# Gate logits as four more columns of A's key projection, read out by GpSimd and spread through DRAM

## The chip, the core and the metric

The kernel runs on one core of a Trainium2 chip. The metric is the device time of one execution in microseconds (us). The kernel is written in Bass with the Tile framework: the program names tiles and engines, the framework adds the semaphore waits that its view of the tiles' reads and writes asks for.

Engines, as the profile names them: PE (TensorE matmuls; PEld its weight loads), DVE (VectorE), ACT (ScalarE), POOL (GpSimd), SP (SyncE, which here only issues transfers). Each executes its instructions in program order. Sums of matmuls land in PSUM, everything else is kept in SBUF.

## What is computed

Two linear-attention blocks, A and B, on the same `x` (2048 rows, 640 columns, 32 heads of 20), mixed by a gate per row:

```
phi(t) = where(t > 0, t + 1, exp(t)) + 1e-6
q, k, v = split(x @ wqkv)               # per block, 32 heads
kv  = phi(k)^T v ;  z = sum over rows of phi(k)
o   = phi(q) kv / (phi(q) z + 1e-6)
block = o @ wo
g   = sigmoid(sum(x * gate_w))          # one logit per row
out = g * A + (1 - g) * B
```

All inputs and the output are bf16.

## The kernel before

The kernel never forms v. It takes G = x^T phi(k) (640x640), then kv = wv^T G per head, multiplies by wo to a 640x640 matrix M per block, and the output is phi(q) M for both blocks, with phi(q) already scaled by the gate and by the reciprocal of the denominator. Rows are taken in 16 chunks of 128 (`ST`), columns in 5 tiles of 128 (`DT`, index c).

The gate comes in through `ge`: geA = 1 + exp(-logit) and geB = 1 + exp(logit). The denominator of block b is multiplied by ge[b] before its reciprocal (L492), which makes the scale of phi(q) equal to g/den for A and (1-g)/den for B. `gate_pass` (L176) makes `ge`: for each half of the rows 20 small matmuls with the gate vector copied to 32 weight columns (`gwr`), in four column groups of PE, so that each group of 32 partitions holds the logits of 256 rows, 32 times over; then two exponentials on ACT and two additions on DVE. That is the layout in which `rec_pass` has the denominators.

Order of work for block A, on the parts that matter here:

- Loads. x's first 512 rows come as four chunks (`load_x`, from SP and ACT), wkA as c = 0, 1, 2 and 3 to 4 together (`load_wk`), then wqA, then the other rows of x by transposing DMAs on SP.
- `k_first` (L222), its order written out by hand: PE transposes the first two x chunks, DVE copies them to xT, PE does k's matmuls of these two chunks for c = 0 and 1, transposes the third chunk, does c = 2 and the third chunk's c = 0 to 2, transposes the fourth, and finishes. `k_mm` does one matmul of 320 columns: a chunk of k has two halves (`hf`), each in a PSUM bank of its own.
- `phi` (L194) takes k or q out of PSUM: ACT writes exp into the tile `e` (three buffers), DVE does min and add on it in place (L200), then add and max with the PSUM source into `pk` or `pqT` (L204). In a "lifted" unit ACT also writes t + 1 into the destination (L199), and DVE's last step reads that instead of PSUM (L202).
- The other k chunks and the q units (`q_unit`, 10 matmuls of 512 columns) alternate; the last part, under a manual schedule, is k chunks 14 and 15, `gwr` widened by DVE between them (L702), then five q units (`q_pass`), of which the last four are lifted, with sums of pk by DVE between (`k_sum`).
- `g_pass` (L278): 32 matmuls of the last c of G. After 12 of them come `z_rows` (z from the sums of pk, 16 matmuls named zA at L388, and DVE's `zr` at L396), `x_sum(1)` (DVE, L502) and `gate_pass` (matmuls named lg); after 14 more `z_pass` (5 matmuls, then DVE's `zsel` at L407). `rec_pass` then makes the denominators (denA) with `zsel` as weights. After it come the rest of G (`g_strassen`) and block B's k, q and G, which go the same way; `ge` is made once and used by both.

PSUM has four slots (`ps`), each of two banks. Without a number, `ps` takes the next slot of a round-robin (`turn`); `g_pass`, `z_rows`, `gate_pass`, `rec_pass` and `g_strassen` name slots 1, 0, 2, 2 and 0/1. Late in the kernel `D3` receives differences of phi(q), from the middle of block B's k stage on (`p_diff`).

SP's queue holds, in order: x, wk and wq loads, 15 transposing loads, the gate vector (640 elements, one to a partition and column), x again in row order, wvA, woA, wkB (waits until A's k is done), wqB (waits until A's q is done), and later transfers.

## Time and profile before

| what | value |
|---|---|
| runs shown | 189.83 us median of 3 (189.77 to 190.37) |
| profiled execution | span 188.1 us, first to last instruction, 3574 instructions; no time of its own is listed beside the span |
| median of the runs less that span | 1.7 us |
| PE / DVE / ACT / POOL busy | 182.7 / 150.3 / 75.0 / 2.8 us |
| granted PE clock over the span | 1.000 |
| matmuls lg (gate logits) | 40, on the chain for 1.09 us from 52.06 us |
| gate exponentials (ACT), additions (DVE) | 2 of 0.60 us, 2 of 0.42 us |

The page of a profile gives the busy time of each engine in the whole span, the span in 40 slices, the chain of work that ended last (followed back from the last instruction to what released each step), the costliest groups of instructions, and the transfers with their time from issue to landing. The trace behind it can be asked for a timeline of a stretch, for the groups by shape, and for who waited for whom. In a timeline a line is: start, length (us), engine, line of the kernel, operation, output<-inputs, shape, count, and in brackets the idle time before it with what ended it. Matmuls overlap, so the pace of a row of them is read from the length of the row by its count and not from the duration of one.

### The profile page before, as it was taken

Reading aid. Unit: us, or ns where it says so; the run is one execution under the profiler, and the core shown is the slowest. Engines: PE = TensorE matmul, PEld = TensorE weight load, DVE = VectorE, ACT = ScalarE, POOL = GpSimd, SP = SyncE. Lnnn points to the kernel's source line nnn. Section 1 sums busy time; section 2 is a strip of 40 time slices with the busy share of each in tenths; the row PEclk is TensorE's granted clock in tenths of the full one; section 3 lists DMA queues with packets and bytes.
Section 4 is the critical chain, followed back from the end, with each engine's and each line's share of the span. In section 5 each row is a group of like instructions: output and inputs, shape, how many; then the busy total and the mean of one; then the engine's idle time right before and its main releaser. Section 6 shows DMA issues by size and latency. Waiting matters only on the chain.

```text
span 188.1 us, 3574 instructions
## 1 busy us (share of the span) xinstructions
PE 182.7 (97%) x1460; PEld 123.5 (66%) x1465; DVE 150.3 (80%) x244; ACT 75.0 (40%) x106; POOL 2.8 (2%) x17
## 2 busy tenths in 40 slices
PE   8899999999999999999999999999999999999992
PEld 3566657755577677877765555576778776777772
DVE  1378968899998999799889997739699989787553
ACT  2055446457942501367674577422401611111110
POOL 6000000000000000000000000000000000000000
PEclk9999999999999999999999999999999999999999
DMA  5975447992140000011115000000543003211222
GB/s 184 320 124 94 105 84 250 360 249 87 16 164 0 3 0 0 3 33 33 54 44 189 2 0 0 3 0 0 178 112 62 3 3 112 97 70 56 87 71 71
DMA packets 19802, 15.63 MB, mean 83 GB/s; under 512 B 9546, under 2 KB 19658, under 8 KB 19786
## 3 DMA queue, kind: packets, MB, share of 16 engines
q1 hardware_dynamic: 18922, 14.59, 29.0%
q10 hardware_dynamic: 864, 0.82, 1.3%
q8 instruction: 11, 0.18, 0.4%
q14 instruction: 5, 0.04, 0.1%
HBM read 10.00 MB, written 3.44 MB: 71 GB/s over the span
## 4 chain that ended last, share of the span: by engine, by line
PE 93%; DMA 3%; DVE 1%; ACTq 0%; issue 0%; ACT 0%; DVEq 0%
PE gs L325 16%; PE kB L207 12%; PE qB L256 11%; PE kA L207 11%; PE qA L256 7%; PE ox L563 6%; PE oy L563 5%; PE oz L563 5%; PE qA L267 5%; DMA xn<-in_A_x_dram 3%; PE ow L563 3%; PE gB L298 2%; PE gA L298 2%; DVE osb L568 1%; PE mA L456 1%; PE mid L417 1%
## 5 line engine op out<-in xcount | busy, mean ns | idle before, releaser
L207 PEld LDWEIGHTS <-xT 128*128 128x128 bf16 x320 | 31.0, 98 | 12.4 <-DVE xT L192 0.5
L200 DVE TENSOR_SCALAR e<-e 128x640 bf16<-128x640 bf16 (+1 forms) x52 | 18.7, 360 | 6.3 <-ACT e L197 5.7
L207 PE MATMUL kB<-wkB,xT 128*128 128x320 bf16 x160 | 23.0, 299 | 0.0
L207 PE MATMUL kA<-wkA,xT 128*128 128x320 bf16 x160 | 22.6, 299 | 0.1
L256 PE MATMUL qB<-xT,wqB 128*128 128x512 bf16 x98 | 21.7, 379 | 0.1
L197 ACT ACTIVATE e<-kB 128x640 bf16<-128x640 f32 x16 | 11.3, 704 | 18.8 <-PE kB L207 17.5
L256 PEld LDWEIGHTS <-wqB 128*128 128x128 bf16 x100 | 11.7, 117 | 9.8 <-issue 0.2
L197 ACT ACTIVATE e<-kA 128x640 bf16<-128x640 f32 x16 | 11.0, 704 | 13.3 <-PE kA L207 13.3
L204 DVE SCALAR_TENSOR_TENSOR pk<-kA,e 128x640 bf16<-128x640 f32 x16 | 13.2, 825 | 1.7
L204 DVE SCALAR_TENSOR_TENSOR pk<-kB,e 128x640 bf16<-128x640 f32 x16 | 13.2, 825 | 1.7
L197 ACT ACTIVATE e<-qA 128x1024 bf16<-128x1024 f32 x10 | 10.2, 1023 | 9.3 <-PE qA L267 3.7
L197 ACT ACTIVATE e<-qB 128x1024 bf16<-128x1024 f32 x10 | 10.2, 1023 | 8.7 <-PE qB L256 8.4
L256 PE MATMUL qA<-xT,wqA 128*128 128x512 bf16 x59 | 13.2, 379 | 0.1
L607 ACT COPY u<-ox 128x320 f32<-128x320 f32 x8 | 3.4, 425 | 21.9 <-PE ox L563 21.9
L325 PEld LDWEIGHTS <-S 128*128 128x128 bf16 x96 | 9.4, 98 | 3.6
L325 PEld LDWEIGHTS <-xn 128*128 128x128 bf16 x96 | 9.1, 98 | 4.0 <-issue 0.4
L256 PEld LDWEIGHTS <-wqA 128*128 128x128 bf16 x60 | 7.0, 117 | 5.8
L563 PEld LDWEIGHTS <-xT 128*128 128x128 bf16 x85 | 8.0, 98 | 3.1 <-DVE xT L502 0.2
L591 ACT COPY p1s<-ox 128x320 f32<-128x320 f32 x8 | 3.4, 426 | 16.6 <-PE ox L563 16.6
L563 PEld LDWEIGHTS <-pqTA 128*128 128x128 bf16 x85 | 7.9, 98 | 2.9 <-issue 0.2
L563 PEld LDWEIGHTS <-pqTB 128*128 128x128 bf16 x80 | 7.8, 98 | 3.0
L325 PE MATMUL gs<-pk,xn 128*128 128x320 bf16 x64 | 9.4, 300 | 0.0
(124 smaller groups left out, 285.2 us busy)
## 6 DMA issues: line engine op xcount, KB each, us to landing
out_dram<-osb SPq DMA_DIRECT2D x14, 160.0 KB, 1.8
xn<-in_A_x_dram SPq DMA_DIRECT2D x3, 640.0 KB, 6.8
wqA<-in_A_wqkv_dram SPq DMA_DIRECT2D x1, 800.0 KB, 7.3
wvA<-in_A_wqkv_dram SPq DMA_DIRECT2D x1, 800.0 KB, 11.8
wkB<-in_B_wqkv_dram SPq DMA_DIRECT2D x1, 800.0 KB, 6.3
wqB<-in_B_wqkv_dram SPq DMA_DIRECT2D x1, 800.0 KB, 4.8
MA<-ma_dram SPq DMA_DIRECT2D x1, 800.0 KB, 4.3
wvB<-in_B_wqkv_dram SPq DMA_DIRECT2D x1, 800.0 KB, 5.7
```

The costliest lines, as they stand in the source:

```text
L197: nc.scalar.activation(out=e[:], in_=src, func=ACT.Exp)
L200: nc.vector.tensor_scalar(e[:], e[:], 1.0, EPS, op0=ALU.min, op1=ALU.add)
L204: nc.vector.scalar_tensor_tensor(out=dst, in0=src, scalar=1.0 + EPS, in1=e[:], op0=ALU.add, op1=ALU.max)
L207: nc.tensor.matmul(pt[:, hf, 0:HF], lhsT=xT[:, c, i * P:(i + 1) * P], rhs=wk[b][:, c, hf * HF:(hf + 1) * HF], start=(c == 0), stop=(c == D ...
L256: nc.tensor.matmul(pt[:, u, :], lhsT=mixed(wq[b][:, c, :], m), rhs=xT[:, c, n * HB:(n + 1) * HB], start=(c == 0), stop=(c == DT - 1),)
L267: nc.tensor.matmul(pt[:, u, :], lhsT=mixed(wq[b][:, c, :], m + u), rhs=xT[:, c, n * HB:(n + 1) * HB], start=(c == 0), stop=(c == DT - 1),)
L298: nc.tensor.matmul(pt[:, hf, 0:HF], lhsT=xn[:, i, c * P:(c + 1) * P], rhs=pk[:, i, hf * HF:(hf + 1) * HF], start=(i == 0), stop=(i == ST - 1),
L325: nc.tensor.matmul(pt[:, n, 0:HF], lhsT=left[:, i, n * P:(n + 1) * P], rhs=right[:, i, :], start=(first and i == 0), stop=(i == hc - 1), s ...
L417: nc.tensor.matmul(pt[:KG, hf, j * KG:(j + 1) * KG], lhsT=wv[b][:, c, (4 * hf + j) * KG:(4 * hf + j + 1) * KG], rhs=GT[hf][:, c, j * KG:(j ...
L563: nc.tensor.matmul(dst, lhsT=left[:, c, r0:r0 + P], rhs=right[:, c, :], start=(first and c == 0), stop=(c == DT - 1), skip_group_check=not ...
L591: nc.scalar.copy(out=self.p1s[:], in_=self.at("x"))
L607: nc.scalar.copy(out=self.u2[:], in_=self.at("x"))
```

## The change

The gate's logits are now made by A's k matmuls. `wk` of A gets four more columns (640 to 643), which hold -gate, gate, -gate, gate; a chunk of k has two halves of 322 columns, and `pk` rows are 644 wide. The columns are made inside `k_first` (`gate_columns`): the gate vector is loaded by GpSimd's queue as 5 rows of 128, a matmul against the identity turns it into a column per c in PSUM (in a corner of the first k chunk's second bank), and two DVE multiplications by -1 and +1 write them into wkA. The exponential that `phi` takes of a k chunk then includes exp(-logit) and exp(logit) of its 128 rows, and GpSimd copies these two columns, cut at 1e30, into `EL` (L225 of the changed kernel). After the second q unit of the last five, `gate_spread` transposes `EL` by a matmul (a PSUM slot of the round-robin), ACT copies it to SBUF, SP writes it to a DRAM scratch, and four transfers read it back, each into 32 partitions with a broadcast, into `EB`, which lies in `D3`. `gate_pass` is left with the two DVE additions. The 40 matmuls, the two exponentials, the widened gate vector and its load are gone.

The diff:

```diff
@@ -28,6 +28,7 @@
 EPS = 1e-6
 RB = 256
 SH = S // 2
+KW = D + 4
 
 
 @with_exitstack
@@ -70,7 +71,7 @@
 
     xT = persist.tile([P, DT, S], BF16, name="xT")
     xn = persist.tile([P, ST, D], BF16, name="xn")
-    pk = persist.tile([P, ST, D], BF16, name="pk")
+    pk = persist.tile([P, ST, KW], BF16, name="pk")
     pqT = [persist.tile([P, DT, S], BF16, name=f"pqT{b}") for b in "AB"]
     GT = [persist.tile([P, DT, HF], BF16, name=f"GT{n}") for n in range(2)]
     KVT = persist.tile([P, 4, 3, KG], BF16, name="KVT")
@@ -84,8 +85,11 @@
     spread = persist.tile([P, P], BF16, name="spread")
     R = persist.tile([P, 2, 4, RB], BF16, name="R")
     ones = persist.tile([P, H], BF16, name="ones")
-    gwr = persist.tile([P, DT, H], BF16, name="gwr")
+    EL = persist.tile([P, 2, ST], BF16, name="EL")
+    ELT = persist.tile([H, P], BF16, name="ELT")
+    g5 = persist.tile([DT, P], BF16, name="g5")
     D3 = persist.tile([P, DT, SH], BF16, name="D3")
+    EB = D3[:, 0, :].rearrange("p (b h r) -> p b h r", b=2, h=2)
     hc, ic = ST // 2, 2 * P
 
     def flat(t, pattern, inner, at=0):
@@ -97,6 +101,7 @@
     SX[4] = flat(M[1], "p c d -> p (c d)", ic)
     TK = [{k: flat(pqT[1], "p c s -> p (c s)", HF, k - 1) for k in (1, 2, 3, 4)}, {}]
     ma_dram = scratch.tile([D, D], BF16, name="ma_dram")
+    gate_dram = scratch.tile([2, S], BF16, name="gate_dram")
     lift = persist.tile([P, 1], FP32, name="lift")
     TM = [persist.tile([P, DT, HF], BF16, name="TM0")] + [None] * 3
     ge = [persist.tile([P, 2 * RB], FP32, name=f"ge{b}") for b in "AB"]
@@ -110,15 +115,17 @@
     nc.vector.memset(lift[:], 1.0 + EPS)
     xb0 = x2[0:CB * P, :].rearrange("(p q) d -> p q d", q=CB)
     wk = [None, None]
+    KF = [KW // 2, HF]
     wv = [None, None]
     wq = [None, None]
-    wk[0] = wpool.tile([P, DT, D], BF16, tag="wk", name="wkA")
+    wk[0] = wpool.tile([P, DT, KW], BF16, tag="wk", name="wkA")
     def load_x(eng, lo, hi):
         eng.dma_start(out=xn[:, lo:hi, :], in_=xb0[:, lo:hi, :])
 
     def load_wk(eng, lo, hi):
-        eng.dma_start(out=wk[0][:, lo:hi, :], in_=wq_dram[0][:, lo:hi, D:2 * D])
-
+        eng.dma_start(out=wk[0][:, lo:hi, 0:D], in_=wq_dram[0][:, lo:hi, D:2 * D])
+
+    nc.gpsimd.dma_start(out=g5[:], in_=gate_w.rearrange("(c p) -> c p", p=P))
     load_x(nc.sync, 0, 1)
     load_x(nc.scalar, 1, 2)
     load_wk(nc.sync, 0, 1)
@@ -129,7 +136,6 @@
     load_x(nc.scalar, 3, 4)
     wq[0] = wpool.tile([P, DT, D], BF16, tag="wq", name="wqA")
     nc.sync.dma_start(out=wq[0][:], in_=wq_dram[0][:, :, 0:D])
-    gcol = persist.tile([P, DT], BF16, name="gcol")
     for n in range(1, NB):
         for c in range(DT):
             nc.sync.dma_start_transpose(
@@ -173,14 +179,33 @@
                     start=(c == 0), stop=(c == DT - 1), tile_position=(0, 32 * j),
                 )
 
+    def gate_columns(pt):
+
+        dst = pt[:, 1, HF + 80:HF + 80 + DT]
+        nc.tensor.matmul(dst, lhsT=g5[:], rhs=ident[:DT, 0:DT], start=True, stop=True)
+        for k, sign in enumerate((-1.0, 1.0)):
+            nc.vector.tensor_scalar(
+                wk[0][:, :, D + k:KW:2], dst[:, :, None].to_broadcast([P, DT, 2]), sign, None, op0=ALU.mult
+            )
+
+    def gate_spread():
+
+        pt = ps("gt")
+        nc.tensor.matmul(pt[:H, 0, 0:P], lhsT=EL[:].rearrange("p b i -> p (b i)"), rhs=ident[:], start=True, stop=True)
+        nc.scalar.copy(out=ELT[:], in_=pt[:H, 0, 0:P])
+        nc.sync.dma_start(out=gate_dram[:].rearrange("b (i p) -> (b i) p", p=P), in_=ELT[:])
+        view = gate_dram[:].rearrange("b (h j r) -> j b h r", h=2, j=4)
+        for j in range(4):
+            nc.sync.dma_start(
+                out=EB[32 * j:32 * j + 32], in_=view[j:j + 1].to_broadcast([32, 2, 2, RB]),
+            )
+
     def gate_pass():
 
-        pt = ps("lg", 2)
-        for h in range(2):
-            by_group(pt[:, 1, h * RB:(h + 1) * RB], gwr, xT, h)
         for b in range(2):
-            nc.scalar.activation(out=ge[b][:], in_=pt[:, 1, :], func=ACT.Exp, scale=(-1.0, 1.0)[b])
-            nc.vector.tensor_scalar(ge[b][:], ge[b][:], 1.0, 1e30, op0=ALU.add, op1=ALU.min)
+            nc.vector.tensor_scalar(
+                ge[b][:], EB[:, b].rearrange("p h r -> p (h r)"), 1.0, 1e30, op0=ALU.add, op1=ALU.min
+            )
 
     def x_transpose(i, slot, eng, cuts=(0, DT)):
         pt = ps_raw("xt", slot)
@@ -191,10 +216,16 @@
         for lo, hi in zip(cuts, cuts[1:]):
             copy(out=xT[:, lo:hi, i * P:(i + 1) * P], in_=src[:, lo:hi])
 
-    def phi(dst, src, n, lifted=False):
+    def phi(dst, src, n, lifted=False, gate=None):
 
         e = work.tile([P, 2, n], BF16, tag="e", name="e", bufs=3)
         nc.scalar.activation(out=e[:], in_=src, func=ACT.Exp)
+        if gate is not None:
+            flat_e = e[:].rearrange("p b n -> p (b n)")
+            nc.gpsimd.tensor_scalar(EL[:, :, gate], flat_e[:, D:D + 2], 1e30, None, op0=ALU.min)
+            nc.vector.tensor_scalar(flat_e[:, 0:D], flat_e[:, 0:D], 1.0, EPS, op0=ALU.min, op1=ALU.add)
+            nc.vector.scalar_tensor_tensor(out=dst, in0=src, scalar=1.0 + EPS, in1=e[:], op0=ALU.add, op1=ALU.max)
+            return
         if lifted:
             nc.scalar.activation(out=dst, in_=src, func=ACT.Identity, bias=lift[:])
         nc.vector.tensor_scalar(e[:], e[:], 1.0, EPS, op0=ALU.min, op1=ALU.add)
@@ -205,12 +236,13 @@
 
     def k_mm(b, i, c, pt, hf):
         nc.tensor.matmul(
-            pt[:, hf, 0:HF], lhsT=xT[:, c, i * P:(i + 1) * P], rhs=wk[b][:, c, hf * HF:(hf + 1) * HF],
+            pt[:, hf, 0:KF[b]], lhsT=xT[:, c, i * P:(i + 1) * P], rhs=wk[b][:, c, hf * KF[b]:(hf + 1) * KF[b]],
             start=(c == 0), stop=(c == DT - 1),
         )
 
     def k_done(b, i, pt):
-        phi(pk[:, i, :].rearrange("p (b n) -> p b n", b=2), pt[:, :, 0:HF], HF)
+        n = KF[b]
+        phi(pk[:, i, 0:2 * n].rearrange("p (b n) -> p b n", b=2), pt[:, :, 0:n], n, gate=None if b else i)
 
     def k_chunk(b, i, slot=None):
         pt = ps(f"k{'AB'[b]}", slot)
@@ -230,6 +262,7 @@
 
         for i in range(2):
             x_transpose(i, i, "dve", (0, 2, DT))
+        gate_columns(pts[0])
         for i in range(2):
             part(i, (0, 1))
         x_transpose(2, 0, "dve", (0, 2, DT))
@@ -660,6 +693,8 @@
 
         for k, (m, h) in enumerate(units):
             q_unit(b, m, h, k in lifted)
+            if b == 0 and k == 1:
+                gate_spread()
             if k in sums:
                 k_sum(b, sums[k])
 
@@ -681,8 +716,6 @@
     q_unit(0, DT - 1, 0)
     for i in range(hc, ST - 2):
         k_chunk(0, i)
-    with nc.allow_non_contiguous_dma(reason="640 elements, one to a partition and column"):
-        nc.sync.dma_start(out=gcol[:], in_=gate_w.rearrange("(c p) -> p c", p=P))
     for n in range(1, NB):
         nc.sync.dma_start(
             out=xn[:, n * CB:(n + 1) * CB, :], in_=x2[n * HB:(n + 1) * HB, :].rearrange("(q p) d -> p q d", p=P)
@@ -699,7 +732,6 @@
 
     with tc.manual_schedule():
         k_chunk(0, ST - 2)
-        nc.vector.tensor_copy(out=gwr[:], in_=gcol[:, :, None].to_broadcast([P, DT, H]))
         k_chunk(0, ST - 1)
         k_sum(0, 1)
         q_pass(0, [(m, 1) for m in range(DT)], {0: 2, 1: 3, 2: 4}, (1, 2, 3, 4))
```

## The prediction

> **What bounds the kernel now.** I read the page first (its busy table), then the chain of waits in order of time, then the timeline of the first 12 us and of the stretch from 49 to 57 us, where the change takes work away.

> ```profile
> PE 182.7 (97%) x1460; PEld 123.5 (66%) x1465; DVE 150.3 (80%) x244; ACT 75.0 (40%) x106; POOL 2.8 (2%) x17
> ```

> TensorE (PE) is busy for 182.7 of 188.1 us. What is put into its queue, taken out of it, or made to wait there is the time; the other engines matter only where they hold it. The chain says so piece by piece (start, length, what):

> ```profile
> 1.73 5.02 DMA xn<-in_A_x_dram
> ...
> 6.79 0.45 PE xt L188 x5
> 7.25 1.37 PE kA L207 x10
> 8.62 0.28 PE xt L188 x5
> 8.90 2.99 PE kA L207 x22
> 11.89 0.21 PE qA L267
> ...
> 49.77 1.63 PE gA L298 x12
> 51.40 0.66 PE zA L388 x16
> 52.06 1.09 PE lg L171 x40
> 53.15 2.01 PE gA L298 x14
> ...
> 56.15 1.21 PE denA L171 x40
> ```

> Up to 6.75 us the chain is a transfer of x; from there to the last output it is nearly all PE, without a gap. So a delay in the first 12 us is handed on whole: no later wait is left that could swallow it. The reader should also see the price tag of what the change removes: the logits (lg) are 1.09 us of the chain.

> **The start, where the new wait is put.** PE's timeline and the weight transfers (line, engine, tile, count, KB, us from issue to landing; the last SP transfer of wkA is issued at 2.2 us):

> ```profile
> 3.90 0.73 PE L188 MATMUL xt<-ident,xn 128*128 128x128 bf16 x10
> 4.77 1.25 PE L207 MATMUL kA<-wkA,xT 128*128 128x320 bf16 x8
> 6.79 0.45 PE L188 MATMUL xt<-ident,xn 128*128 128x128 bf16 x5 [0.77 <-DMA xn<-in_A_x_dram]
> ```

> ```profile
> wkA<-in_A_wqkv_dram SPq DMA_DIRECT2D x1, 320.0 KB, 5.7
> ```

> Before, eight matmuls of k run at 4.77 us on the first weight rows that have landed (c = 0 and 1), and PE then sits 0.77 us for the third x chunk. The rows c = 3 and 4 land at 2.2 + 5.7 = 7.9 us, and nobody minds, since they are first wanted at 8.9 us.

> gate_columns puts a small matmul and two VectorE (DVE) multiplications between the transposes and those eight matmuls. The multiplications write two columns of every weight row, with a stride of 644. In the instruction list of the built kernel the first of them carries waits on three DMA counters: those on which the k matmuls of c = 1, of c = 2 and of c = 3 wait. It does so although it touches no column that these transfers write: its strided write spans them. And the first k matmul now waits for DVE, where before it waited for its own weights alone; the later k matmuls and the transposes of chunks 2 and 3 stand behind it in PE's queue, the copies of those transposes behind it in DVE's. So k starts not at 4.77 us but after the landing at 7.9.

> The sum for the start: 7.9 for the landing; two DVE multiplications of 128x10 out of PSUM. No row shows this form: the DVE line constant is bounded by 0.06 us (memset of 128x1) and 0.23 (mask product of 80x80 from PSUM), and I take 0.15 each, near the latter since it also reads PSUM: 8.2; a hand-over of 0.05 as between landing and xt (6.75 to 6.79): 8.25. Eight matmuls at the steady pace of this stage (2.99 us for 22, so 0.136): 1.09, done at 9.35. From the transposes of the third chunk on, the order is as before, which took 6.79 to 11.89; they now begin at 9.35 instead of 6.79: **+2.56 us**. x chunks 2 and 3 have landed by then, so the old wait of 0.77 is inside this figure. It would fall to +0.06 if only true dependences counted: DVE ends its fourth copy at 5.4, the multiplications at 5.7, k starts at 5.76 and the eight end at 6.85 against 6.79.

> What of the start costs nothing beside that: the load of the five gate rows, now first on GpSimd's queue, whose cost no row shows. It pushes the identity's building (0.80 to 1.53 us on POOL) back; the transposes need it at 3.90, and up to 7.9 any delay of either is under the wait. The longest landing after issue in this stage is the 5.7 us above; issued at about 0.8 it lands by 6.5, under 7.9 too. If the wait did not exist, both would be bare. ScalarE's table load (1.28 us) may also be held until DVE is done; it then ends near 9.5, and the first exponential is due only near 12.

> **k's wider tiles.** 160 matmuls of kA go from 320 to 322 columns: at 0.136 us for 320, 0.85 ns each, **+0.13 us** with all of it on the path. ScalarE's exponentials (704 ns, 16) and DVE's maxima (825 ns) grow by 4 columns of about 1 ns: per chunk under 0.01 us, beside PE's 1.36. The 16 GpSimd copies of 128x2 are new; nearest rows are its copies of 32x32 (203 ns) and memsets of 128x1 (100 ns). They run beside DVE's first step on the same buffer. If each held DVE up by its full 0.2 us, the stretch 28 to 39 us (8 chunks, DVE 9.5 busy of 11.0) has 0.19 us a chunk to give: nothing on PE, or at worst a few tenths where DVE runs without a gap, from 39.6 us. The removed widening of the gate vector (0.31 us) gives DVE as much back there. Taken as zero, bounds -0.1 and +0.3.

> **The spread.** One matmul with 32 weight columns and 128 moving ones after the second q unit: at the pace of the transposes (0.28 for 5) 0.06, with its wait for a slot **+0.08 us**. ScalarE's copy of 32x128 (about 0.28, since 320 columns take 0.43 and 640 0.70) falls between exponentials that have about 0.13 us of air per unit; it is worked off within two units. Five transfers go through SP ahead of wqB's load: written near 46 us and, at the landing times of this size (output stores of 160 KB 1.8 us), back by 51, wanted by DVE at 54.4. What is queued behind them, wqB, is issued at 49.8 now and first read at 98: no cost. The removed 2-byte load of the gate was in no one's way.

> **The logits' place.** Minus 40 matmuls: -1.09 us. But two things take most of it back. First, the spread's PSUM slot moves all later ones by one. By the round-robin of four, the last q unit then sits in slot 0, which z_rows takes; before, it sat in slot 3. The built kernel's first zA matmul indeed waits for ScalarE, where before it waited for DVE only.

> ```profile
> 50.73 1.11 ACT L199 ACTIVATE pqTA<-qA,lift 128x1024 bf16<-128x1024 f32 x1
> ```

> This is the last q unit's read of its slot, ending at 51.84: zA starts at 51.9, not 51.40: +0.49. Second, DVE sets zsel, on which the denominators wait:

> ```profile
> 52.90 0.49 DVE L396 TENSOR_TENSOR zr<-zA,zu 128x320 bf16<-128x320 f32 x1
> 53.30 1.22 DVE L502 TENSOR_TENSOR S<-xn 128x2048 bf16<-128x2048 bf16 x1
> 54.44 0.42 DVE L183 TENSOR_SCALAR geA<-geA 128x512 f32<-128x512 f32 x1
> 54.77 0.42 DVE L183 TENSOR_SCALAR geB<-geB 128x512 f32<-128x512 f32 x1
> 55.44 0.32 DVE L407 TENSOR_TENSOR zsel<-zA,headE 128x160 bf16<-128x160 f32 x1 [0.25 <-PE zA L403]
> ```

> PE alone would reach the denominators at 56.15 - 1.09 + 0.49 = 55.55. zr comes 0.8 us behind the end of zA (52.06 to 52.90), so now at 53.1 to 53.4; the same four steps end zsel 2.6 us later, 55.7 to 56.0, and the denominators start some 0.05 after. Against 56.15 that leaves 0.1 to 0.4: **-0.2 us**, and nothing if DVE takes longer on bf16 logits than its 0.42. Without these two it would be the whole -1.09.

> **Sum.** +2.56 + 0.13 + 0.08 - 0.2 = +2.57 on the span of 188.1, so 190.7. No time is listed for the profiled execution beyond its span; the median of the runs, 189.83, is 1.7 above it, and I keep that: **192.4 us**. About 0.3% (0.57 us) is what a measurement of this kernel can tell from no change.

> **Rivals.** *The clock falls back.* PE would stand from 4.65 to 8.25, 3.6 us. The seven warm-up matmuls run at 631 ns each against 379 for later ones of the same size, so the clock does start low here and rises near 3.7 us; the profile shows no PE gap of this length between two matmuls, so it does not say whether it would hold. If it halves until 3.4 us of matmuls have run (as long as the warm-up needed, 0.84 to about 3.7, and somewhat more), those 3.4 us do half the work: +1.7, or 194.1; if the first rise is itself missed, up to 194.7. [...] Chance 0.15.

> *Faster: the wait is not there and the slot is free.* If the wide transfer's landing comes before DVE arrives (5.4 us; it decides from there on, one us of time for each us of landing), the start costs 0.06; if zA and zsel are also not held, the total is 0.06 + 0.13 + 0.08 - 1.09 = -0.8: 189.0. For it: the columns really are disjoint. Against: the waits in the instruction list, and a landing that would have to come 2.5 us sooner with the same bytes ahead of it. Chance 0.04.

> *Wait gone, slot and DVE as reckoned:* +0.07, 189.9, no change that can be told. Chance 0.03. *A partial wait* (landing near 6.5 to 7): 191. Chance 0.08.

> **Numbers.** The forecast, 192.4, has 0.70, with a range of its own from 191.6 to 193.2 (landing +-0.3, DVE's steps, the last unknowns). The range 191.3 to 194.4 takes in it and most of the clock case. Slower: 0.70 + 0.15 + 0.08 = 0.93; same 0.03; faster 0.04.

> **What would show it.** Right: on PE's timeline a gap from about 4.7 to 8.2 us that ends with DVE's write of wkA, and that write released by a wkA transfer; kA's first exponential near 12; every later stage 2.5 us later; zA released by ScalarE; denA starting 0.1 to 0.4 us sooner after qA than now. Wrong: k matmuls before 7 us, or a clock below full after 8 us.

## The result, and the profile after

The changed kernel takes 195.42 us (median of 6 runs, 194.01 to 195.72) against 189.96 us before (6 runs): ratio 1.026, 95% interval 1.023 to 1.030. The forecast, 192.4, had the sign and the place, but its range ended at 194.4. The profiled execution took 195.62 us with a span of 193.8, 5.7 more than before.

From the page of the changed kernel, the busy row and the granted clock over 40 slices of 4.8 us:

```profile
PE 184.7 (95%) x1427; PEld 123.6 (64%) x1427; DVE 150.2 (78%) x245; ACT 74.1 (38%) x105; POOL 7.8 (4%) x34
...
PEclk9759999999999999999999999999999999999999
```

PE has 33 matmuls fewer in the record than before and is busy 2 us longer, because its clock is below full in the second and third slice. The timeline of the start, PE's lines and DVE's write of the gate columns:

```profile
3.71 0.73 PE L213 MATMUL xt<-ident,xn 128*128 128x128 bf16 x10
...
4.92 0.17 PE L185 MATMUL kA<-ident,g 5*128 5x5 bf16 x1 [0.47 <-DMA g<-in_gate_w_dram]
...
8.58 0.26 DVE L187 TENSOR_SCALAR wkA<-kA 128x10 bf16<-128x10 f32 x2 [3.36 <-DMA wkA<-in_A_wqkv_dram]
8.89 2.31 PE L238 MATMUL kA<-wkA,xT 128*128 128x322 bf16 x8 [3.80 <-DVE wkA L187]
```

DVE stands 3.36 us for a transfer of wkA, PE 3.80 us for DVE: the wait that the prediction named, with k at 8.89 us instead of 4.77. Then eight matmuls take 2.31 us where the pace at full clock is 0.136 each, 1.1 in all. The same stretch by windows (length, busy times of the engines, granted clock, DMA share, GB/s):

```profile
3.70:4.45 0.75, 0.75 (x11) 0.56 (x10) 0.24 (x2) 0.00 (x0) 0.64 (x4) 1.00 1.07 251
4.45:8.89 4.44, 0.17 (x2) 0.18 (x2) 1.03 (x6) 0.00 (x0) 0.40 (x2) 0.77 0.96 319
8.89:11.20 2.31, 2.31 (x10) 1.37 (x10) 0.00 (x0) 1.28 (x1) 0.00 (x0) 0.50 1.34 207
11.20:13.70 2.50, 2.50 (x14) 1.56 (x13) 0.56 (x2) 0.00 (x0) 0.00 (x0) 0.50 0.70 144
13.70:17.44 3.74, 3.74 (x31) 2.74 (x30) 1.97 (x5) 1.91 (x3) 0.89 (x3) 1.00 0.44 98
```

The clock had risen, fell within the gap, and came back at 13.7 us only. A mean of 0.77 over 4.44 us is 0.46 x 4.44 = 2.0 us at half speed, so it fell near 6.9, about 2.4 us after the last transpose. From the first k matmul to the first of q it is 8.55 us (8.89 to 17.44). The chain of waits shows the later stages:

```profile
44.64 4.32 PE qA L289 x20
48.96 0.16 PE gt L194
49.12 6.62 PE qA L289 x30
...
56.78 1.01 ACT pqTA L230
57.79 0.04 issue
57.84 0.73 PE zA L421 x16
...
61.61 0.33 DVE zsel L440
61.94 0.04 issue
61.98 1.27 PE denA L177 x40
```

The five q units take 11.10 us with the spread's matmul (10.79 before), zA is released by ACT's read of the last q unit, denA by DVE's zsel. Where the 5.7 us of the span went: q starts at 17.44 instead of 11.89 (+5.55); the 120 later k matmuls +0.11 (10.94 for 80, 10.87 before, and 5.47 for 40, 5.43 before); the five q units +0.31; from the end of q to denA 6.24 instead of 6.38 (-0.14); the rest -0.1.

### The profile page after: what moved, and what is told of

Same layout as the page of the kernel before. It is cut to its first block, busy times and chain, and to the rows that moved or that the text cites. A ratio compares the mean times of both kernels' runs of the same rounds, so it can differ in the third digit from the quotient of the medians.

```text
span 193.8 us, 3531 instructions
## 1 busy us (share of the span) xinstructions
PE 184.7 (95%) x1427; PEld 123.6 (64%) x1427; DVE 150.2 (78%) x245; ACT 74.1 (38%) x105; POOL 7.8 (4%) x34
## 4 chain that ended last, share of the span: by engine, by line
PE 91%; DMA 3%; DVE 2%; ACT 1%; SPq 1%; issue 0%; DVEq 0%; ACTq 0%
PE gs L358 16%; PE kA L238 12%; PE kB L238 11%; PE qB L289 11%; PE qA L289 7%; PE ox L596 6%; PE oy L596 5%; PE oz L596 5%; PE qA L300 4%; DMA wkA<-in_A_wqkv_dram 3%; PE ow L596 2%; PE gB L331 2%; PE gA L331 1%; DVE osb L601 1%; PE mA L489 1%; PE mid L450 1%
## 5 line engine op out<-in xcount | busy, mean ns | idle before, releaser
L238 PEld LDWEIGHTS <-xT 128*128 128x128 bf16 x320 | 31.8, 100 | 17.2 <-issue 3.8
L238 PE MATMUL kA<-wkA,xT 128*128 128x322 bf16 x160 | 24.8, 316 | 3.8 <-DVE wkA L187 3.8
L231 DVE TENSOR_SCALAR e<-e 128x1024 bf16<-128x1024 bf16 (+1 forms) x36 | 13.6, 379 | 5.4 <-ACT e L222 5.0
L222 ACT ACTIVATE e<-kA 128x644 bf16<-128x644 f32 x16 | 11.1, 707 | 12.7 <-PE kA L238 12.0
L227 DVE SCALAR_TENSOR_TENSOR pk<-kA,e 128x644 bf16<-128x644 f32 x16 | 13.3, 829 | 2.1 <-PE kA L238 0.5
L289 PE MATMUL qA<-xT,wqA 128*128 128x512 bf16 x60 | 13.5, 379 | 0.0
L596 PEld LDWEIGHTS <-xT 128*128 128x128 bf16 x85 | 8.0, 98 | 3.0 <-DVE xT L535 0.2
```

Of the source, the lines that this page charges most:

```text
L222: nc.scalar.activation(out=e[:], in_=src, func=ACT.Exp)
L227: nc.vector.scalar_tensor_tensor(out=dst, in0=src, scalar=1.0 + EPS, in1=e[:], op0=ALU.add, op1=ALU.max)
L231: nc.vector.tensor_scalar(e[:], e[:], 1.0, EPS, op0=ALU.min, op1=ALU.add)
L238: nc.tensor.matmul(pt[:, hf, 0:KF[b]], lhsT=xT[:, c, i * P:(i + 1) * P], rhs=wk[b][:, c, hf * KF[b]:(hf + 1) * KF[b]], start=(c == 0), sto ...
L289: nc.tensor.matmul(pt[:, u, :], lhsT=mixed(wq[b][:, c, :], m), rhs=xT[:, c, n * HB:(n + 1) * HB], start=(c == 0), stop=(c == DT - 1),)
L596: nc.tensor.matmul(dst, lhsT=left[:, c, r0:r0 + P], rhs=right[:, c, :], start=(first and c == 0), stop=(c == DT - 1), skip_group_check=not ...
```

## The experiments

**Row-by-row columns.** The corner of PSUM is copied to SBUF, and each weight row gets its two columns by instructions of its own, written just before the matmuls that need them:

```diff
-        for k, sign in enumerate((-1.0, 1.0)):
-            nc.vector.tensor_scalar(wk[0][:, :, D + k:KW:2], dst[:, :, None].to_broadcast([P, DT, 2]), sign, ...)
+        nc.vector.tensor_copy(out=gsb[:], in_=dst)
+    def gate_rows(cs):
+        for c in cs:
+            for k, sign in enumerate((-1.0, 1.0)):
+                nc.vector.tensor_scalar(wk[0][:, c, D + k:KW:2], gsb[:, c:c + 1].to_broadcast([P, 2]), sign, ...)
...
         gate_columns(pts[0])
+        gate_rows((0, 1))
...
         x_transpose(2, 0, "dve", (0, 2, DT))
+        gate_rows((2,))
...
         x_transpose(3, 0, "dve")
+        gate_rows((3, 4))
```

> The changed kernel, with the gate columns written row by row: the corner of PSUM is copied out to SBUF at once, and the two columns of a weight row are written by DVE instructions of 128x2 just before the k matmuls that read them, so that no write spans the transfer of the rows c = 3 and 4 before PE needs these. Theory 1 (what the change lost is lost at the start: the wait for that transfer, and the clock that falls during it): the gap on PE before the first k matmul shrinks from 3.8 us to about 0.5 to 1, the clock stays at full speed, and the time comes back to 190.0 to 190.6, the kernel before plus 0.1 for the start, 0.14 for the wider k, 0.3 for the spread's matmul, less 0.15 at the logits. Theory 2 (GpSimd beside DVE, the wider tiles and the transfers through DRAM cost it): these are all still there, and the time stays at 194 to 195.7.

Measured: 192.56 us (6 runs), ratio to the kernel before (190.31 beside it) 1.013, interval 1.010 to 1.015. Over half of the loss is gone with GpSimd's copies, the wide tiles and the DRAM transfers all in place, which theory 2 does not allow; but it missed the expected time by 2 us. PE's timeline says why:

```profile
5.76 1.41 PE L244 MATMUL kA<-wkA,xT 128*128 128x322 bf16 x8 [0.61 <-DVE gsb L187]
...
8.24 1.40 PE L244 MATMUL kA<-wkA,xT 128*128 128x322 bf16 x9 [0.66 <-DVE wkA L193]
...
10.64 3.04 PE L244 MATMUL kA<-wkA,xT 128*128 128x322 bf16 x21 [0.59 <-DVE wkA L193]
```

The long wait has become three short ones. My placing put the column writes of c = 2 and of c = 3 and 4 behind the copies of the next x chunk, on which these matmuls had never waited. q starts at 13.69, 1.8 us later than before the change.

**The filled gap.** The wait is kept, and PE is given work in it:

```diff
         gate_columns(pts[0])
+        for k in range(16):
+            nc.tensor.matmul(pts[1][:, 0, :], lhsT=one_l, rhs=one_r, start=True, stop=True)
```

> The changed kernel with 16 more matmuls of 128x512 on constants, whose results are never read, behind the gate matmul, so that PE works for about 3.4 us of the 3.8 in which it waits. The wait itself is as it was. Theory 1 with the clock (a gap in which the clock falls): the clock stays at full speed, k starts at about 8.9 us as in the changed kernel, and its first 40 matmuls take half the time: 193.0 to 193.4, some 2.2 below the longer runs of the changed kernel and 0.8 below its shorter ones. If the clock has no part (the wait and slower transfers alone): 194 to 195.7 as before.

Measured: 193.24 us (4 runs, 192.97 to 193.85), ratio 1.015 (1.013 to 1.018). From its timeline and its windows:

```profile
5.04 3.67 PE L267 MATMUL kA<-const-bfloat16-1.0 128*128 128x512 bf16 x16
9.34 1.27 PE L238 MATMUL kA<-wkA,xT 128*128 128x322 bf16 x8 [0.62 <-DVE wkA L187]
```

```profile
4.50:9.30 4.80, 4.22 (x23) 1.97 (x21) 1.27 (x6) 0.00 (x0) 0.35 (x2) 1.00 1.01 314
9.30:12.00 2.70, 2.66 (x23) 1.88 (x23) 0.56 (x2) 1.28 (x1) 0.00 (x0) 1.00 1.37 172
```

k starts later than in the changed kernel (9.34 against 8.89; the transfer came 6.7 us after issue, not 6.3), and yet q starts at 15.57, 1.9 us sooner. From the first k matmul to q it is 6.23 us here, 8.55 in the changed kernel: the fallen clock cost 2.3 us, by a run that keeps the wait and gives PE work in it. The windows of the changed kernel say the same: 4.83 us of matmuls at half speed (8.89 to 13.72) lose 2.4. What is left at the start, 5.55 - 2.3 = 3.2, is the wait.

**The start alone.** The gate columns, their load and the wide k stay; GpSimd's read-out, the spread and the DRAM transfers go, and the logits are taken as before the change (`gate_pass` with its 40 matmuls, `gwr` and `gcol` back in place).

> One part alone: the gate columns, their load, their two wide writes and the 322-column k, but no read-out by GpSimd, no spread and no transfers through DRAM; the logits are taken as in the kernel before (40 matmuls, two exponentials, the widened vector). Theory 1: the whole loss is there: 193.9 to 195.6. Theory 2 (GpSimd's copies, the spread): close to the kernel before, 190 to 190.5.

Measured: 196.44 us (4 runs, 195.50 to 196.91), ratio 1.032 (1.029 to 1.035). The whole loss is there, and 0.8 us above what I expected. In the profiled execution, its shortest run, the wide transfer of wkA came 6.8 us after issue, 0.5 later than in the changed kernel's profile; q starts at 16.89. Here the clock is back sooner. PE's line and the windows before and after the clock's return are:

```profile
9.40 2.30 PE L237 MATMUL kA<-wkA,xT 128*128 128x322 bf16 x8 [4.22 <-DVE wkA L185]
```

```profile
9.40:12.03 2.63, 2.63 (x13) 1.69 (x13) 0.00 (x0) 1.28 (x1) 0.00 (x0) 0.50 1.19 168
12.03:16.89 4.86, 4.86 (x40) 3.45 (x39) 2.52 (x7) 1.91 (x3) 0.00 (x0) 1.00 0.54 115
```

From the first k matmul to q it is 7.49 us, 1.3 more than with the gap filled: the clock's price was 1.3 us in this execution and 2.3 in the changed kernel's. The longer runs left no trace to read, and why they are longer than the changed kernel's stays open.

**Ten narrow writes, still out of PSUM.** The wide pair is cut into ten of 128x2 in the same place:

```diff
-        for k, sign in enumerate((-1.0, 1.0)):
-            nc.vector.tensor_scalar(wk[0][:, :, D + k:KW:2], dst[:, :, None].to_broadcast([P, DT, 2]), sign, ...)
+        for c in range(DT):
+            for k, sign in enumerate((-1.0, 1.0)):
+                nc.vector.tensor_scalar(wk[0][:, c, D + k:KW:2], dst[:, c:c + 1].to_broadcast([P, 2]), sign, ...)
```

> The changed kernel with only its two wide writes cut into ten of 128x2, one row at a time, in the same place and still out of PSUM. Of the ten, only those of c = 3 lie inside the span of the late transfer. If the first k matmul waits for the wide writes themselves, it can now start near 5.9 us. If it waits for the reading of the PSUM corner, which lies in the tile that it writes, it stands behind the last of the ten reads, and so behind the late transfer as before: k at about 9, the clock falls, 194 to 196.

Measured: 196.05 us (one run; 190.25 for the kernel before beside it). DVE's timeline and PE's:

```profile
5.33 0.49 DVE L188 TENSOR_SCALAR wkA<-kA 128x2 bf16<-128x2 f32 x6
8.61 0.36 DVE L188 TENSOR_SCALAR wkA<-kA 128x2 bf16<-128x2 f32 x4 [2.79 <-DMA wkA<-in_A_wqkv_dram]
```

```profile
9.03 2.31 PE L239 MATMUL kA<-wkA,xT 128*128 128x322 bf16 x8 [3.93 <-DVE wkA L188]
```

The columns of c = 0 to 2 are written by 5.8 us, and k still starts at 9.03, half clock and all. So two dependences lie one behind the other: the writes of c = 3 wait for a transfer that they only lie inside of, and the first k matmul waits for the last read of the PSUM corner, since that corner is in the tile that it writes. Copying the corner out removes the second: in the kernel with row-by-row columns the copy ends at 5.70 and the first k matmul starts at 5.76, while the four column writes ahead of it in program order still run, until 6.12. The first is still seen in the kernel with the start in another order (below): DVE stands 0.25 us for that transfer there, and PE does not wait for it.

**The slot.** On the row-by-row kernel, the spread moved after the first q unit, with its slot by name:

```diff
-        pt = ps("gt")
+        pt = ps("gt", 1)
...
-            if b == 0 and k == 1:
+            if b == 0 and k == 0:
```

> As the kernel with row-by-row columns, and the spread comes after the first of the five q units instead of the second, in PSUM slot 1 by name, so that the round-robin stays as before the change and z_rows no longer takes the last q unit's slot. If the slot is what holds zA (my reckoning, 0.49 us), zA starts right behind the first 12 matmuls of G, and the denominators about 0.4 us sooner than in the kernel with row-by-row columns: 189.7 to 190.2. If DVE alone sets the denominators, zA moves and the denominators do not: the same time as that kernel within 0.1.

Measured: 191.59 us (6 runs), ratio 1.008 (1.005 to 1.011). The median is 0.97 us below the row-by-row kernel's, but the two intervals overlap. In its trace zA follows the first 12 matmuls of G without a stop, and G's start to denA takes 5.71 us (53.48 to 59.19); in the row-by-row kernel it takes 6.24 (51.99 to 58.23). Freeing the slot, with the earlier place of the spread, is worth 0.53 us at the denominators. PE still stands 0.40 us for DVE's zsel ahead of them, so both holds of the prediction are real, and the slot is the larger. The absolute time was not as expected, for the start had not been mended. The profiled execution, the longest of the six with 193.07 us, lost more at the start than the row-by-row kernel did:

```profile
5.91 2.32 PE L244 MATMUL kA<-wkA,xT 128*128 128x322 bf16 x8 [0.58 <-DVE gsb L187]
```

These eight matmuls run at half pace, where the same line of the row-by-row kernel has 1.41. The windows print a clock of 1.00 there, but the clock record of this trace begins only at 9.99 us (in the other traces at 3.5 to 5.8): the first rise came late, and before it the record is empty. The comparison from G's start on is not touched by this.

**The start in another order.** On top of this, PE does the first half of chunk 0 ahead of the gate matmul, and DVE writes columns ahead of later copies:

```diff
-        gate_columns(pts[0])
-        gate_rows((0, 1))
-        for i in range(2):
-            part(i, (0, 1))
+        def half(i, hf):
+            for c in (0, 1):
+                k_mm(0, i, c, pts[i], hf)
+
+        half(0, 0)
+        gate_columns(pts[1])
+        gate_rows((0, 1, 2))
+        half(1, 0)
+        half(0, 1)
+        half(1, 1)
         x_transpose(2, 0, "dve", (0, 2, DT))
-        gate_rows((2,))
+        gate_rows((3, 4))
...
         x_transpose(3, 0, "dve")
-        gate_rows((3, 4))
```

> Row-by-row columns again, with the spread after the first q unit in a slot of its own, and the start put in another order: PE does the first chunk's first half of c = 0 and 1 ahead of the gate matmul, DVE writes the columns of c = 0, 1 and 2 in one go and those of c = 3 and 4 before it copies the fourth x chunk, so that no k matmul stands behind a column write that stands behind a later copy. If the 1.5 us that the first row-by-row kernel still lost in k_first are such hand-overs, q starts at 12.0 to 12.4 us (11.9 before the change), the clock does not fall, and the time is 190.0 to 190.6 beside 190.3 of the kernel before on this chip. If the loss belongs to the wider k or to GpSimd, q starts no earlier than the 13.5 us of the first row-by-row kernel and the time stays near 191.6.

Measured: 190.21 us (12 runs) beside 190.25 before, ratio 1.000 (0.998 to 1.002). Its timeline:

```profile
4.90 0.72 PE L244 MATMUL kA<-wkA,xT 128*128 128x322 bf16 x2
5.55 0.18 PE L186 MATMUL kA<-ident,g 5*128 5x5 bf16 x1
5.99 0.98 PE L244 MATMUL kA<-wkA,xT 128*128 128x322 bf16 x6 [0.26 <-DVE gsb L187]
6.81 0.44 PE L219 MATMUL xt<-ident,xn 128*128 128x128 bf16 x5
```

q starts at 11.94 (11.89 before the change): all of the 5.5 us at q's start was in how the columns were put in, none in what they are used for.

**DVE's order at the logits.** On top again, the addition for block B goes behind A's reciprocals:

```diff
-    def gate_pass():
+    def gate_pass(bs):
...
-        for b in range(2):
+        for b in bs:
...
-                    gate_pass()
+                    gate_pass((0,))
...
         rts = rec_pass(b, zsel, 2)
+        if b == 0:
+            gate_pass((1,))
```

> As the kernel with the early order, and the second addition (geB, which only block B reads) is moved behind A's reciprocals, so that zsel comes 0.35 us sooner on DVE. If DVE's order is what still holds the denominators (0.39 us of wait on zsel), they start 0.3 to 0.4 us sooner and the time falls by as much: 189.6 to 190.2, below the kernel before by up to 0.5. If the reciprocals, which DVE does next, set the pace anyway, the same as the kernel with the early order.

Measured: 190.19 us (12 runs), ratio 0.998 (0.996 to 1.001). In the trace G's start to denA is 5.38 us (49.54 to 54.92), 0.34 less than the 5.72 of the kernel with the early order, as expected; in the time the step is not told from nothing. No version was found that beats the kernel before by more than the runs can tell.

## Why the prediction was wrong, step by step

- *The wait for the wide transfer: right in kind, short by 0.7 us.* Predicted +2.56 at full clock, measured 3.2. The transfer landed 6.3 us after issue, not 5.7 (8.45 us), DVE took it up at 8.58, and k started at 8.89 instead of 8.25. The two DVE writes took 0.26 together, 0.30 in the sum. My 0.3 of room for the landing was too small: in the profiles of the four kernels that write the columns straight out of PSUM it came 6.3 to 6.8 us after issue, in those of the four that copy the corner out first 5.6 to 5.9. Why it comes later in the former, no run shows.
- *That the clock would hold: the step that failed.* The forecast gave its falling a chance of 0.15 and a price of 1.7 to 2.3 us. It fell in the profiled execution, and the price, by the filled gap, is 2.3; where it came back sooner, in the profile of the start alone, it is 1.3. The mean clock is below full in five of the six runs: three at 0.982 took 195.55 to 195.72 us, two at 0.991 took 194.0. The sixth reads 1.000 and took 195.28. It left no trace, so its length is not explained; a first rise that comes late, which the forecast named within this rival, would not show in the mean, as the slot's profile tells. That the clock would hold through the gap, and the 0.15, were the author's estimate; no run had shown it. The fall came 2.4 us after the last transpose, in a stretch of 3.41 us since the clock's rise (3.48 to 6.89, shown in the last section) in which PE had worked for 1.14, on the end of the warm-up, transposes and one tiny matmul. The forecast's 3.4 us of matmuls until the clock is back was an estimate from the warm-up (2.9 us, 0.84 to about 3.7) and shown by no run before the change: in the changed kernel it took 4.83 (8.89 to 13.72), in the start alone 2.63 (9.40 to 12.03). The fall should have been in the sum and not a rival. Even with it at the forecast's price the time would have been 194.1 to 194.7: the wait and the spread were short as well, and 2.3, 0.7 and 0.2 come to 3.2 us, about the 3.1 that the sum lacked on the span.
- *The spread's matmul: 0.31 us for the q units, predicted 0.08.* The matmul itself has 0.16 in the chain. PEld is idle 0.41 us ahead of its 32-column weight load, which the full-width loads around it do not show; I priced the pace of a row, not the break in it. That this break is the rest of the 0.31 is argued; no run takes it apart.
- *The wider k: +0.13 predicted*, 0.11 measured for three quarters of it. Right.
- *The logits' place: -0.2 predicted, -0.14 measured*, with both holds as named: zA late by the slot (0.47 by the chain, 0.49 in the sum), zsel by DVE. DVE takes 0.42 on bf16 logits as on fp32.
- *GpSimd beside DVE, taken as zero: right.* DVE's first step on `e` takes 319 ns as a mean over A's 16 chunks, 321 before over the 32 of both blocks.
- *The gate load bare or covered: covered.* It landed at 4.9 us; the identity was done at 2.7. The sum took 5.7 us for the longest landing of this stage, and that was misread: in the same profile wqA's 800 KB took 7.3. It did no harm, for the gate vector took 3.6.
- *The transfers through DRAM: covered.* The last was issued by 54.4 us, and DVE's read at 60.94 does not wait.

## What to carry to other kernels

With this framework, a strided write into a tile whose other columns are still being loaded can be made to wait for every load that its span crosses, and a corner borrowed in an accumulator tile makes its next writer wait for the last read: read the waits in the built kernel's instruction list, and give small values a tile of their own. For a new wait on PE like this one, put the fallen clock into the sum and not among the accidents: in all three profiles here in which PE stood for 3.80 to 4.22 us ahead of k the clock fell, and it cost 2.3 us in the changed kernel, where the wait itself cost 3.2, and 1.3 in the start alone. Taking 1.09 us off PE's queue brought 0.1, because a shifted PSUM slot and DVE's order held the next step; moved work has to be followed to what is late next.

## What the runs showed of the hardware

The changed kernel's clock fell although PE had worked for 1.14 of the 3.41 us before. These are the windows between the changes in the clock record, three of the changed kernel and, last, one of the start alone:

```profile
3.48:6.89 3.41, 1.14 (x13) 0.75 (x12) 1.02 (x4) 0.00 (x0) 1.22 (x6) 1.00 0.95 277
6.89:10.31 3.42, 1.42 (x6) 0.83 (x6) 0.26 (x2) 1.28 (x1) 0.00 (x0) 0.50 1.17 293
10.31:13.72 3.41, 3.41 (x18) 2.11 (x17) 0.56 (x2) 0.00 (x0) 0.00 (x0) 0.50 0.86 169
8.62:12.03 3.41, 2.63 (x13) 1.69 (x13) 0.26 (x2) 1.28 (x1) 0.00 (x0) 0.50 1.47 202
```

GpSimd's copy of 128x2 takes 0.21 us alone and 0.33 to 0.38 in six of 16 cases, when DVE's 0.32 us step on the same buffer starts with it (GpSimd's timeline; DVE's step for the second line runs from 42.77 to 43.09):

```profile
41.41 0.21 POOL L225 TENSOR_SCALAR EL<-e 128x2 bf16<-128x2 bf16 x1 [1.15 <-ACT e L222]
42.78 0.38 POOL L225 TENSOR_SCALAR EL<-e 128x2 bf16<-128x2 bf16 x1 [1.15 <-ACT e L222]
```

In these six the copy is 0.12 to 0.17 us longer and ends 0.07 to 0.08 us behind DVE's step, which takes 0.32 to 0.33 us beside a copy as without one: here it is GpSimd that gives way, and DVE loses nothing. Why, the trace does not show.
